# Two transfers per chunk instead of six for the last heads' rows, two closing stores on ScalarE, new planner numbers

## The chip, the cores and the metric

The kernel runs on one core of a Trainium2 chip. TensorE (PE in the profile) multiplies, VectorE (DVE) and ScalarE (ACT) work elementwise and empty PSUM, GpSimd (POOL) works elementwise on SBUF, SyncE (SP) issues nearly all transfers. The metric is the device time of one execution in microseconds, as the median of three runs. The kernel before took 326.67 us (326.44 to 327.48).

## The reference

Two computations in a row, for 4 batches of 768 positions. First a gated linear attention with 8 heads of 48 channels:

```
for t in range(S):
    state = alpha[:, :, t, :, None] * state + einsum('bhd,bhe->bhde', k[:, :, t], v[:, :, t])
    y[:, :, t] = einsum('bhd,bhde->bhe', q[:, :, t], state)
```

Its output, heads side by side (384 columns), is the input x of the second: four causal softmax attentions of width 64 ("experts"), each with its own wq, wk, wv, wo. A gate `x @ w_gate` picks two of the four for each position and weighs them.

```
scores = scale * (q @ k.transpose(0, 2, 1))          # causal mask, softmax -> a
ye = a @ v @ wo[e]
out += mask[..., None] * w[:, :, kk:kk + 1] * ye     # for the two experts chosen
```

## The kernel before

The sequence is cut into 24 chunks of 128 positions (6 for each batch). Three chunks make a unit u, two units a batch. A chunk n goes through these steps: SP loads alpha (`al`), q and k (`T`) and `v`; DVE turns alpha into running products with two scans (`prep_r`, `prep_c`, both through L163) and multiplies k and q with them (L182, L187); PE makes the products of the chunk (`gla_a`, L206), transposes k (`gla_t`, L223), makes the state's update (`gla_u`, L243) and the output (`gla_y`, L282). The masks between `gla_a` and `gla_y` are made either by DVE alone (L210) or by ACT and then POOL (L214, L218). A unit then goes through projections (`proj`, L305; `vproj`, L327), scores (L378), row maxima and exponentials (L390, L401), scaling on POOL (L413), transposes (L428), the product with v (L453) and the output product (`outp`, L472), whose result is copied to one of two `ot` tiles and stored (L480).

Heads lie in pairs on the partitions: one head on rows 0 to 47, the other on 64 to 111. From chunk 3 on (`FIRST = 3`) only three of the four pairs are loaded densely. The rows of the last two heads ride in the rows that are left over, 16 in each of three tiles, so that DVE prepares three tiles and not four. `spread` (L189) then moves them with transfers from SBUF to SBUF into their own, fourth tile: six transfers for each chunk, issued by SP (L194). PE's products of the fourth pair, and POOL's scaling of the state (L260), wait for them.

The order of all instructions is made by a planner at build time (`op` and `run`). Each step has a key, the steps it depends on, the engines that could do it with an assumed cost, and a target time. `run` takes, engine by engine, the step that can begin soonest, corrected by how far its target lies ahead. The targets come from PACE (assumed time of a chunk) and the shifts in OFF. Where a step may go to DVE or to another engine, the planner decides that too. Where it expects PE to be idle for longer than IDLE, it puts in filler products (`warm`, L805). So new numbers give a new order on every engine. Each queue runs strictly in its order: an instruction that waits holds back all behind it.

At the very end the count of a check (L856 to L864) decides whether a slow second path is taken; each engine loads it (`cnt`, TENSOR_LOAD at L864) before it goes on. On ACT this load stands ahead of the last copy of an output tile.

Of the kernel before, what the change touches and what calls it, by code (L numbers as in the profile page):

```python
# [17 lines left out]
B, H, S, D = 4, 8, 768, 48  # L18
DM = H * D
NE, HD = 4, 64  # L20
C = 128
# [9 lines left out]
TINY = 1.0e-12  # L31

FIRST = 3
PACE = 12.6339
PULL = {"P": 0.007, "V": 0.02, "A": 0.02, "G": 0.1134, "S": 0.1114}
SWITCH = 0.6006
CHANGE = {("t", "f"): 0.065, ("f", "t"): 0.0}
# [2 lines left out]
CHANGE.update({(x, "y"): 0.12 for x in "tfas"})  # L40
CHANGE.update({(x, "t"): 0.15 for x in "asy"})
CHANGE.update({(x, "f"): 0.2 for x in "asy"})
IDLE = 0.3068
SHARE = 0
HEAD = 0.0374
MARGIN = 0.3816
SLOW = 1.056
OFF = dict(load=1.5592, prep=0.7084, a=-0.2534, y=0.0569, p=-0.066, pw=0.4525, v=-0.5128, g=0.5234, s=-0.069, step=0.925, n=0.3117, tr=1.0059, o=0.1922, w=0.6642, wt=-1.9145, hp=1.0622, ck=0.4, end=1.3946, hd=0.0189, sx=-0.1743, wo=0.3118, xo=-0.0467)
UNITS = dict(a=7, at=4, ms=2, kt=2, x=2, q=3, k=4, yy=2, vg=3, T=4, al=3, v=3, ot=2, st=2)
HAND = {("P", "V"): 0.2, ("P", "A"): 0.2, ("P", "G"): 0.2, ("V", "P"): 0.1, ("A", "P"): 0.1, ("G", "P"): 0.14, ("S", "P"): 0.1,  # L50
        ("V", "G"): 0.07, ("A", "G"): 0.07, ("G", "V"): 0.07, ("G", "A"): 0.07}
# [4 lines left out]
def tile_gla_moe(ctx: ExitStack, tc: tile.TileContext, qk_d, al_d, v_d, wqk_d, wv_d, wo_d, nat_d, vn_d, out_d):  # L56
    nc = tc.nc
    V, A, G, PE, SY = nc.vector, nc.scalar, nc.gpsimd, nc.tensor, nc.sync
# [33 lines left out]
    wo = view(raw[2][:, 780:780 + 2 * DM], 2, DM)  # L92
# [66 lines left out]
    cq, ck = slice(0, 256), slice(256, 512)  # L159
# [29 lines left out]
    def spread(n):  # L189
        t = at(("T", n))  # L190
        for s in (0, 64):
            for i in range(3):
                r = s + 16 * i
                SY.dma_start(t[r:r + 16, 3, 0:2 * C + 1], t[s + D:s + 64, i, 0:2 * C + 1])  # L194

    def check(n):
        x = al(n).rearrange("p i a w -> p (i a w)") if n else raw[0][:, 0:8 * CW]
# [286 lines left out]
    def op(key, target, deps, alts, uses=(), take=(), mode="", land=0.0, lock=False):  # L484
        o = dict(key=key, target=target, deps=list(deps), alts=alts, uses=list(uses), take=list(take), mode=mode, land=land, lock=lock)
        ops.append(o)
        for n in o["uses"]:
            users[n] = users.get(n, 0) + 1
        return o
# [7 lines left out]
    def either(f, n, *a):  # L497
        return [("A", da(n), lambda: f("A", *a)), ("V", dv(n), lambda: f("V", *a))]

    def load_ops(n):  # L500
        z = (n - 3 - OFF["load"]) * PACE
        if n > HALF:
# [8 lines left out]
    def prep_ops(n):  # L511
        z = (n - 2 - OFF["prep"] + OFF["hp"] * max(0.0, 1.0 - (n - HALF) / 3) * (n >= HALF)) * PACE
        for i, (p0, p1) in enumerate(pieces(n)):
            k = p1 - p0
            past = [("c", n - 2, 0)] if n > 1 else []
            op(("r", n, i), z, [("La", n, i)] + past, [("V", 0.33 + 0.27 * k, lambda i=i: prep_r(n, i))], [("al", n)], lock=True)
            op(("e", n, i), z, [("r", n, i), ("Lq", n, i)], [("G", 0.19, lambda i=i: prep_e(n, i))], [("al", n), ("T", n)])
            op(("c", n, i), z, [("r", n, i)], [("V", 0.15 + 0.27 * k, lambda i=i: prep_c(n, i))], [("al", n)], lock=True)
            op(("k", n, i), z, [("r", n, i), ("Lq", n, i)], scale(prep_k, 128 * k, n, i), [("al", n), ("T", n)],
               lock=True)  # L520
            op(("q", n, i), z, [("c", n, i), ("Lq", n, i)], scale(prep_q, 128 * k, n, i), [("al", n), ("T", n)],
               lock=True)
        ready = [(x, n, i) for x in "ekq" for i in range(len(pieces(n)))]
        if n >= FIRST:
            op(("cp", n), z, ready, [("S", 3.45, lambda: spread(n))], [("T", n)], land=2.2)
            ready = [("cp", n)]
        op(("ck", n), z + OFF["ck"] * PACE, [(x, n, i) for x in "ekq" for i in range(len(pieces(n)))],
           [("A", 0.28 + 0.0021 * 129 * tiles(n) * 0.8, lambda: check(n))], [("al", n)])
        return ready

    def chunk_ops(n):
# [4 lines left out]
        head = OFF["hd"] if n < HALF else 0.0  # L536
        z = (n - 1 + OFF["a"] - head) * PACE
        op(("a", n), z, ready, [("P", 0.95, lambda: gla_a(n))], [("T", n)], [("pa", n, 0), ("pa", n, 1), ("ms", n)], "a")
# [5 lines left out]
        if not last:  # L544
            op(("t", n), z, ready, [("P", 0.42, lambda: gla_t(n))], [("T", n)], [("pt", n)], "t")
            op(("kt", n), z, [("t", n)], either(gla_k, 448, n), [("pt", n)], [("kt", n)])
        z = (n + OFF["y"] - head) * PACE
        op(("y", n), z, [("m", n, 0), ("m", n, 1), ("Lv", n)] + ([("S", n)] if c else []),
           [("P", 1.55 if c else 0.95, lambda: gla_y(n))], [("T", n), ("v", n), ("ms", n)], [("py", n)], "y")
        zx = z + OFF["xo"] * PACE  # L550
        op(("xh", n), zx, [("y", n)], [("A", da(W3), lambda: gla_xh(n))], [("py", n), ("x", u)], [("x", u)] if g == 0 else [])
# [39 lines left out]
    def back_ops(u):  # L591
        b, hf = divmod(u, 2)
        c = HALF * u + HALF
        tail = u == NU - 1
        step = (0.3333 + 0.3333 * hf) * OFF["step"]
        base = c + OFF["s"]
        seq = [(pair, i) for pair in (0, 1) for i in range(3)]
        for k, (pair, i) in enumerate(seq):
            tiles3 = [i] if hf else [0, 1, 2]
            first = hf or i == 0  # L600
            z = (base + step * k) * PACE
# [18 lines left out]
            for e in (0, 1):  # L620
                w = [c1 - c0 for c0, c1 in widths(u, i)]
                t = (u, pair, i, e)
# [5 lines left out]
            n = 128 * (3 * hf + i + 1)  # L628
            for e in (0, 1):
                t = (u, pair, i, e)  # L630
                op(("ns",) + t, z, [("n", u, pair, i), ("g3", u)], [("G", 0.35 + 0.00083 * n, lambda a=t: norm_s(*a))], [probs[e]])
            z = (base + step * k + OFF["tr"]) * PACE
            for e in (0, 1):
                t = (u, pair, i, e)
# [7 lines left out]
            if i == 2 or (tail and pair):  # L642
                for i0, i1 in ([(i, i + 1)] if tail and pair else [(0, 3)]):
                    z = (base + step * (k + 1) + OFF["o"]) * PACE
# [3 lines left out]
                    n = 128 * (i1 - i0)  # L648
                    y = ("yy", u, pair)
# [8 lines left out]
        for i in range(3):  # L658
            z = (base + step * 6 + OFF["w"] + 0.1 * i) * PACE
            op(("w", u, i), z, [("ol", u, 0, 0, 3), ("ol", u, 1, i, i + 1) if tail else ("ol", u, 1, 0, 3)],  # L660
               [("P", 1.06, lambda i=i: outp(u, i))], [("yy", u, 0), ("yy", u, 1)], [("po", u, i)], "f")
            end = tail and i == 2
            op(("wo", u, i), z, [("w", u, i)] + [("good",)] * end, either(outp_o, DM, u, i)[:1 if end else 2], [("po", u, i), ("ot", u, i)], [("ot", u, i)])
            op(("st", u, i), z, [("wo", u, i)], [("A", 0.4, lambda i=i: store(A, u, i)) if end else
                                                ("S", 0.57, lambda i=i: store(SY, u, i))], [("ot", u, i)], land=2.2)

# [31 lines left out]
    def run(start, arrive):  # L698
# [31 lines left out]
        while todo:  # L730
# [46 lines left out]
            alt[2]()  # L777
            dur = alt[1] * (SLOW if e in "VAG" else 1.0)
            end = t + dur
# [79 lines left out]
    z = (NG + 4) * PACE  # L859
# [5 lines left out]
    good = []  # L865
# [5 lines left out]
    with tc.If(good[0] == 0):  # L871
# [12 lines left out]
        for c in range(S // TT):  # L884
# [12 lines left out]
            for x in range(0, TT * D, 512):  # L897
                o = unit["g"][x // 512 % 8]
# [39 lines left out]
def _pack(q, k, v, alpha, w_gate, wq, wk, wv, wo):  # L938
    import numpy as np
    f = np.float32  # L940

    def pairs(x, fill, rev):
        x = x.reshape(B, 4, 2, NC, C, D)
        if rev:
            x = x[:, :, :, :, ::-1]
        x = x.transpose(0, 1, 2, 5, 3, 4)
        o = np.full((B, 4, 128, NC, C), fill, f)
        o[:, :, 0:D] = x[:, :, 0]
        o[:, :, 64:64 + D] = x[:, :, 1]
        for i in range(3):  # L950
            o[:, i, D:64] = x[:, 3, 0, 16 * i:16 * i + 16]
            o[:, i, 64 + D:128] = x[:, 3, 1, 16 * i:16 * i + 16]
        return o

    qf, kr, af, ar = pairs(q, 0, False), pairs(k, 0, True), pairs(alpha, 1, False), pairs(alpha, 1, True)
    qk = np.stack([x.transpose(0, 3, 2, 1, 4) for x in (qf, kr)], axis=4).reshape(NG, 128, 4, 2 * C)
    al = np.zeros((NG, 128, 2, 4, CW), f)
    for i, x in enumerate((af, ar)):
        al[:, :, i, :, 1:] = x.transpose(0, 3, 2, 1, 4).reshape(NG, 128, 4, C)
    vr = v.reshape(B, 4, 2, NC, C, D)[:, :, :, :, ::-1].transpose(2, 0, 3, 4, 1, 5)  # L960
    vp = np.zeros((B, NC, C, 4, 128), f)
    vp[..., 0:D] = vr[0]
    vp[..., 128 - D:128] = vr[1]
    vp = vp.reshape(B, NC, C, 512)
    nat = np.stack([x.reshape(B * H, S // 32, 32, 4, 12).transpose(1, 3, 0, 2, 4) for x in (alpha, k, q)], axis=3)
    nat = nat.reshape(S // 32, 128, 3 * 32 * 12)
    vn = v.reshape(B * H, S * D)
    rows = np.zeros((3, 4, 32), np.int64)
    for h in range(H):
        p, s = divmod(h, 2)  # L970
        rows[h // 4, h % 4] = h * D + 16 * s + np.arange(32)
        rows[2, p, 16 * s:16 * s + 16] = h * D + (32 if s == 0 else 0) + np.arange(16)
    rows = rows.reshape(3, 128)

    def wcols(*ws):
        w = np.concatenate(ws, axis=1)
        return np.ascontiguousarray(w[rows].transpose(1, 0, 2))

    wqk = wcols(*[wq[e] for e in range(NE)], *[wk[e] for e in range(NE)])
    wvg = wcols(*[wv[e] for e in range(NE)], w_gate)  # L980
    wop = np.ascontiguousarray(wo.reshape(2, 2 * HD, DM).transpose(1, 0, 2))
    return [np.ascontiguousarray(x) for x in (qk, al, vp, wqk, wvg, wop, nat, vn)]
# [27 lines left out]
```

## Time and profile before

| | us |
|---|---|
| median of 3 runs | 326.67 |
| profiled execution | 327.29 |
| its span, first to last instruction | 325.6 |
| PE busy | 310.3 |
| DVE busy | 266.6 |
| ACT busy | 196.9 |
| POOL busy | 129.5 |

The profiled execution lasts 327.29 us, of which 325.6 us lie between its first and last instruction. "Busy" of PE is a model: products overlap, and the end of each is worked out. A row of the timeline gives start and duration, and in brackets how long the engine sat idle before it and for what. The granted clock of PE was 1.00 in all slices but the last.

### The profile page before, as it was taken

The page shows a single profiled execution, that of the slowest core. Times are in us where ns is not written, and L with a number is a line of the kernel's source. Part 1 is how long each engine was busy: PE and PEld are TensorE (multiplying, and loading weights), DVE is VectorE, ACT ScalarE, POOL GpSimd, SP SyncE. Part 2 cuts the span into 40 slices and gives each one's busy share as a digit, 9 for nine tenths or more (in the row PEclk, how much of TensorE's full clock was granted, in tenths as well). Part 3 has the DMA queues.
Part 4 walks back from the last instruction along what each step waited for, and adds up shares of the span by engine and source line. Part 5 has one row for each costly group of instructions (what it writes and reads, how often), then busy time and mean ns, then how long its engine had stood idle before and what let it go on. Part 6 is the DMA issues. An engine that isn't in the chain of part 4 may idle for free.

```text
span 325.6 us, 11354 instructions
## 1 busy us (share of the span) xinstructions
PE 310.3 (95%) x4447; PEld 265.2 (81%) x4447; DVE 266.6 (82%) x754; ACT 196.9 (60%) x544; POOL 129.5 (40%) x202
## 2 busy tenths in 40 slices
PE   7799989999999999999999999999999999999992
PEld 5678877789887987889897987799897887878682
DVE  5998989999999899889899899599995785277740
ACT  1562655757665675656585777356584775457851
POOL 6353328512655073606455084205463072105320
PEclk9999999999999999999999999999999999999998
DMA  7994255373351321626353220713310000201001
GB/s 253 395 333 139 75 150 158 105 214 99 122 177 58 113 86 21 199 71 199 95 182 104 60 83 23 235 34 132 113 48 9 2 3 2 73 2 66 9 28 58
DMA packets 27982, 35.22 MB, mean 108 GB/s; under 512 B 3632, under 2 KB 24208, under 8 KB 27920
## 3 DMA queue, kind: packets, MB, share of 16 engines
q1 hardware_dynamic: 27232, 33.69, 32.5%
q8 instruction: 37, 0.61, 0.8%
q10 hardware_dynamic: 688, 0.72, 0.7%
q14 instruction: 25, 0.20, 0.2%
HBM read 27.61 MB, written 4.72 MB: 99 GB/s over the span
## 4 chain that ended last, share of the span: by engine, by line
PE 73%; DVE 13%; DMA 4%; ACT 2%; issue 2%; SPq 2%; POOL 1%; DVEq 0%; POOLq 0%; ACTq 0%
PE g L305 12%; PE g L428 11%; PE g L453 11%; PE g L378 9%; PE g L282 8%; PE g L472 7%; PE g L327 6%; PE g L206 5%; DVE al L163 2%; DMA T<-T 2%; PE g L243 2%; SPq L194 2%; DVE a L163 2%; PE g L223 2%; DVE T L182 1%
## 5 line engine op out<-in xcount | busy, mean ns | idle before, releaser
L413 POOL TENSOR_SCALAR a<-a,cf,gw 128x128 f32<-128x128 f32 (+5 forms) x96 | 75.4, 795 | 77.7 <-DVE cf L407 38.0
L401 ACT ACTIVATE a<-a,mx 128x256 f32<-128x256 f32 (+3 forms) x96 | 51.4, 538 | 7.0 <-DVE mx L390 6.9
L428 PE MATMUL g<-ident,a 128*128 128x128 f32 x336 | 52.6, 277 | 0.3
L305 PE MATMUL g<-x,wqkh 128*128 128x384 f32 x192 | 51.8, 350 | 0.3
L428 PEld LDWEIGHTS g<-ident,a 128*128 128x128 f32 x336 | 38.8, 140 | 7.9 <-issue 4.1
L227 ACT ACTIVATE at<-g 128x512 f32<-128x512 f32 (+3 forms) x79 | 34.9, 454 | 13.5 <-PE g L428 12.8
L218 POOL TENSOR_SCALAR_AFFINE_SELECT ms<-ms 128x512 f32<-128x512 f32 x25 | 18.0, 729 | 59.0 <-ACT ms L214 57.2
L453 PE MATMUL g<-at,vg 128*32 128x384 f32 (+2 forms) x648 | 40.2, 389 | 0.0
L378 PE MATMUL g<-k,q 64*128 64x256 f32 (+3 forms) x384 | 39.2, 336 | 0.0
L453 PEld LDWEIGHTS g<-at,vg 128*32 128x32 f32 x648 | 19.8, 110 | 18.5 <-issue 14.9
L282 PE MATMUL g<-ms,v 128*32 128x128 f32 x768 | 33.5, 274 | 0.9 <-DVE mx L390 0.4
L305 PEld LDWEIGHTS g<-x,wqkh 128*128 128x128 f32 x192 | 33.2, 189 | 1.1 <-DVE x L296 0.4
L378 PEld LDWEIGHTS g<-k,q 64*128 64x128 f32 x384 | 28.6, 185 | 5.8 <-issue 2.4
L327 PE MATMUL g<-wvh,x 128*128 128x260 f32 x144 | 31.9, 297 | 0.6 <-DVE mx L390 0.5
L305 PE MATMUL g<-x,wqkl 128*128 128x384 f32 x96 | 32.5, 338 | 0.0
L206 PE MATMUL g<-T 48*128 48x128 f32 x384 | 26.5, 277 | 3.3 <-DVE T L187 3.2
L229 DVE COPY at<-g 128x512 f32<-128x512 f32 (+3 forms) x49 | 24.0, 495 | 6.4 <-PE g L428 6.0
L390 DVE CUSTOM_DVE_ANT_0 a<-g,cmask 128x128 f32<-128x128 f32 (+3 forms) x64 | 28.0, 483 | 1.0 <-PE g L378 0.9
L206 PEld LDWEIGHTS g<-T 48*128 48x128 f32 x384 | 24.1, 188 | 5.3 <-DVE T L187 4.1
L472 PE MATMUL g<-woh,yy 128*128 128x384 f32 x96 | 27.3, 346 | 0.0
L260 POOL TENSOR_TENSOR S<-st,T 48x192 f32<-48x192 f32 x32 | 20.0, 626 | 17.4 <-DMA T<-T 6.5
L198 ACT ACTIVATE al<-al 128x774 f32<-128x774 f32 x21 | 17.8, 850 | 13.2 <-DVE T L187 10.3
(113 smaller groups left out, 636.8 us busy)
## 6 DMA issues: line engine op xcount, KB each, us to landing
al<-in_al_dram SPq DMA_DIRECT2D x21, 387.0 KB, 4.3
T<-in_qk_dram SPq DMA_DIRECT2D x21, 384.0 KB, 4.5
v<-in_v_dram SPq DMA_DIRECT2D x24, 256.0 KB, 3.4
out_dram<-ot SPq DMA_DIRECT2D x23, 192.0 KB, 1.9
T<-T SPq DMA_DIRECT2D x126, 16.1 KB, 1.9
a<-in_al_dram SPq DMA_DIRECT2D x2, 516.0 KB, 7.1
T<-in_qk_dram SPq DMA_DIRECT2D x2, 512.0 KB, 7.2
at<-in_wqk_dram SPq DMA_DIRECT2D x1, 768.0 KB, 9.2
```

Source lines behind the costliest of these rows:

```text
L206: PE.matmul(pa[s][:, C * p:C * p + C], t[r:r + D, p, C:2 * C], t[r:r + D, p, 0:C], start=True, stop=True, tile_position=(r, 0))
L227: A.activation(out, src, AF.Copy)
L282: PE.matmul(o[32 * j:32 * j + 32, k], l, r, start=(i == 0), stop=(i == len(parts) - 1), tile_position=(0, 32 * j))
L305: PE.matmul(pj[:, :W3], w[:, kt, cs], x[:, kt, :], start=(i == 0), stop=(i == 8))
L327: PE.matmul(pv[:, 0:260], x[:, kt, 128 * i:128 * i + 128], w[:, kt, :], start=(m == 0), stop=(m == 8))
L378: PE.matmul(sc(u, pair, i, e, x, c1 - c0), q[r, i0, ts], k[r, i1, c0:c1], start=(y == 0), stop=(y == 2), tile_position=(64 * e, 0))
L390: V.tensor_tensor_reduce(a[:, c0:c1], src, cmask[:, 512 - c1 + c0:512], -1.0, mx[:, 0:1] if x else 3.0e38, OP.add, OP.min, mx[:, 1:2])
L401: A.activation(a[:, c0:c1], src, AF.Exp, bias=mx[:, 1:2], scale=-1.0 if last else 1.0, accum_out=sm[:, x:x + 1])
L413: G.tensor_scalar(a[:, 0:n], a[:, 0:n], CF[u % 2][:, 3 * pair + i, e:e + 1], gw[:, u, i, eg:eg + 1], op0=OP.mult, op1=OP.mult)
L428: PE.transpose(pt[:, 128 * (j - j0):128 * (j - j0) + 128], a[:, 128 * j:128 * j + 128], ident)
L453: PE.matmul(o[r:r + 32, lo:n1], v[:, j % 3, 64 * eg + x:64 * eg + x + 32], at(("at", u, pair, e))[:, min(j, 4), at_off(j) + lo:at_off(j) + ...
L472: PE.matmul(po[:, 0:DM], y[:, h, 128 * i:128 * i + 128], w[:, pair, :], start=(m == 0), stop=(m == 5))
```

## The change

There are three edits. The first: `spread` issues two transfers for each chunk, one for each of the last two heads, and each moves 48 rows. The host packs these rows so that every third one lies in the same tile (`i::3` instead of blocks of 16), and one transfer with a plain order of rows does it. The planner's cost for the step on SP goes from 3.45 to 1.15 us. The second: of the last unit's three output tiles not only the last but the last two are copied by ACT and stored by ACT. The third: PACE, IDLE, HEAD, MARGIN, SLOW and some shifts in OFF have new values, so the order changes on all engines.

```
-PACE = 12.6339
+PACE = 12.4037
...
         for s in (0, 64):
-            for i in range(3):
-                r = s + 16 * i
-                SY.dma_start(t[r:r + 16, 3, 0:2 * C + 1], t[s + D:s + 64, i, 0:2 * C + 1])
+            SY.dma_start(t[s:s + D, 3, 0:2 * C + 1], t[s + D:s + 64, 0:3, 0:2 * C + 1])
...
-            op(("cp", n), z, ready, [("S", 3.45, lambda: spread(n))], [("T", n)], land=2.2)
+            op(("cp", n), z, ready, [("S", 1.15, lambda: spread(n))], [("T", n)], land=2.2)
...
-            end = tail and i == 2
-            op(("wo", u, i), z, [("w", u, i)] + [("good",)] * end, either(outp_o, DM, u, i)[:1 if end else 2], [("po", u, i), ("ot", u, i)], [("ot", u, i)])
+            end = tail and i > 0
+            op(("wo", u, i), z, [("w", u, i)] + [("good",)] * (end and i == 2), either(outp_o, DM, u, i)[:1 if end else 2], [("po", u, i), ("ot", u, i)], [("ot", u, i)])
...
-            o[:, i, D:64] = x[:, 3, 0, 16 * i:16 * i + 16]
-            o[:, i, 64 + D:128] = x[:, 3, 1, 16 * i:16 * i + 16]
+            o[:, i, D:64] = x[:, 3, 0, i::3]
+            o[:, i, 64 + D:128] = x[:, 3, 1, i::3]
```

The lines behind `spread` stand two lower in the new kernel (L192 for L194, L478 for L480); this text uses the numbers of before.

SP, chunks 3 to 5 (T_88, T_85, T_86 are their q and k tiles). Before:

```order
L109 DMA T_87<-in_qk_dram 128x3x256
L194 DMA T_88<-T_88 16x257 x6
L105 DMA al_89<-in_al_dram 128x2x387
L194 DMA T_85<-T_85 16x257 x6
L105 DMA al_90<-in_al_dram 128x2x387
L194 DMA T_86<-T_86 16x257 x6
```

And now:

```order
L109 DMA T_87<-in_qk_dram 128x3x256
L192 DMA T_88<-T_88 48x1x257 x2
L105 DMA al_89<-in_al_dram 128x2x387
L192 DMA T_85<-T_85 48x1x257 x2
L105 DMA al_90<-in_al_dram 128x2x387
L192 DMA T_86<-T_86 48x1x257 x2
```

The order there is the same, with two issues in each place instead of six; over the kernel 126 issues become 42.

DVE, the scans of chunk 3 (al_89; wol is the low part of the output weights). Before:

```order
L163 SCALAR_TENSOR_TENSOR al_89<-al_89,d1r 128x387
L169 RECIPROCAL d1c_110<-al_89 128x3
L163 SCALAR_TENSOR_TENSOR al_89<-al_89,d1c_110 128x387
L182 TENSOR_TENSOR T_88<-T_88,al_89 128x3x128
L187 TENSOR_TENSOR T_88<-T_88,al_89 128x3x128
```

And now:

```order
L163 SCALAR_TENSOR_TENSOR al_89<-al_89,d1r 128x387
L169 RECIPROCAL d1c_110<-al_89 128x3
L666 TENSOR_TENSOR wol<-at_65,woh 128x768
L163 SCALAR_TENSOR_TENSOR al_89<-al_89,d1c_110 128x387
L182 TENSOR_TENSOR T_88<-T_88,al_89 128x3x128
L187 TENSOR_TENSOR T_88<-T_88,al_89 128x3x128
```

The subtraction that makes wol came from POOL, where it stood beside these scans, to DVE between them.

ACT, the end of the main path (ot_95, ot_96 are the last two output tiles). Before:

```order
L459 ACTIVATE yy_81<-g_104 128x128
L227 ACTIVATE ot_95<-g_107 128x384
L864 TENSOR_LOAD cnt
L227 ACTIVATE ot_96<-g_106 128x384
L480 DMA out_dram<-ot_96 128x384
```

And now:

```order
L457 ACTIVATE yy_81<-g_107 128x128
L225 ACTIVATE ot_95<-g_105 128x384
L478 DMA out_dram<-ot_95 128x384
L862 TENSOR_LOAD cnt
L225 ACTIVATE ot_96<-g_102 128x384
L478 DMA out_dram<-ot_96 128x384
```

The store of ot_95 now stands between its copy and the load of the count, ahead of the last copy.

On PE the useful instructions are the same in number; the fillers (L805) go from 77 to 73. Of the places where the kind of product changes there were 295 in the main path and are now 302. In the stretch after the third value product of unit 0, five fillers and the products of chunk 3 (L206) follow at once, where a projection (L305) came first. The transposes of chunk 4 (L223) and its state update (L243) stand ahead of its products (L206), where the update came behind them. In the main path DVE makes 19 masks (23 before) and ACT with POOL 29 (25 before); 16 more copies out of PSUM go to DVE.

## Rows read from the trace of the kernel before

**Rows 1.** The page: busy time of each engine, and DVE's busy tenths in 40 slices
```profile
PE 310.3 (95%) x4447; PEld 265.2 (81%) x4447; DVE 266.6 (82%) x754; ACT 196.9 (60%) x544; POOL 129.5 (40%) x202
DVE  5998989999999899889899899599995785277740
```

**Rows 2.** Waits of PE: line, for whom, us in total, times, longest
```profile
PE g L223 <- DMA T<-T: 0.7, 1, 0.7
...
PE g L327 <- DVE mx L390: 0.5, 1, 0.5
```

**Rows 3.** Chain that ended last, one place in two batches: start, us, what
```profile
157.46 1.54 PE g L282 x56
...
231.18 1.54 PE g L282 x56
```

**Rows 4.** Timeline of PE, 33 to 63 us: start, us, instruction, idle before
```profile
33.24 0.52 PE L305 MATMUL g<-x,wqkh 128*128 128x384 f32 x2
...
34.84 0.72 PE L805 MATMUL g<-d1r 128*128 128x256 bf16 x5
35.49 1.71 PE L206 MATMUL g<-T 48*128 48x128 f32 x16
...
42.50 0.29 PE L223 MATMUL g<-ident,T 112*128 112x112 f32 x1 [0.72 <-DMA T<-T]
...
44.04 1.05 PE L206 MATMUL g<-T 48*128 48x128 f32 x16
45.78 0.54 PE L243 MATMUL g<-v,kt 128*32 128x48 f32 x32 [0.68 <-ACT ms L214]
46.25 1.16 PE L206 MATMUL g<-T 48*128 48x128 f32 x16
...
50.41 0.49 PE L805 MATMUL g<-d1r 128*128 128x256 bf16 x3
...
62.30 1.07 PE L282 MATMUL g<-ms,v 128*32 128x128 f32 x30 [0.23 <-POOL ms L218]
```

**Rows 5.** Timeline of SP's issues, 31 to 35 us
```profile
31.62 3.78 SPq L194 DMA_DIRECT2D T<-T  x6
```

**Rows 6.** Timeline of POOL, 27 to 37 us
```profile
27.99 1.82 POOL L668 TENSOR_TENSOR wol<-at,woh 128x768 fp32r<-128x768 f32 x1
...
36.76 0.70 POOL L260 TENSOR_TENSOR S<-st,T 48x192 f32<-48x192 f32 x1 [1.03 <-DMA T<-T]
```

**Rows 7.** Timeline of DVE, 22 to 34 us
```profile
22.54 0.95 DVE L668 TENSOR_TENSOR wqkl<-at,wqkh 128x768 fp32r<-128x768 f32 x1
...
28.03 2.61 DVE L163 TENSOR_TENSOR_SCAN al<-al,d1c 128x387 f32<-128x387 f32 x1
...
32.67 0.96 DVE L163 TENSOR_TENSOR_SCAN al<-al,d1c 128x387 f32<-128x387 f32 x1
```

**Rows 8.** Timelines of SP, ACT and PE around a unit's stores, 195 to 210 us
```profile
195.16 8.66 SPq L194 DMA_DIRECT2D T<-T  x12
...
208.64 0.49 ACT L227 ACTIVATE ot<-g 128x384 f32<-128x384 f32 x1 [3.38 <-DMA out_dram<-ot]
...
209.56 1.03 PE L305 MATMUL g<-x,wqkh 128*128 128x384 f32 x2
```

**Rows 9.** Timeline of ACT from 318 us, and ACT's load of the count
```profile
318.54 0.49 ACT L227 ACTIVATE ot<-g 128x384 f32<-128x384 f32 x1 [0.98 <-PE g L472]
319.58 0.49 ACT L227 ACTIVATE ot<-g 128x384 f32<-128x384 f32 x1 [0.55 <-PE g L472]
320.10 0.37 ACTq L480 DMA_DIRECT2D out_dram<-ot  x1
...
L864 ACTq TENSOR_LOAD <-cnt x1: 467/467/467, 318.6 to 318.6; - x1
```

**Rows 10.** POOL: all masks by line and form (count, busy, mean ns, idle), and one pair of scalings
```profile
L218 POOL TENSOR_SCALAR_AFFINE_SELECT ms<-ms 128x512 f32<-128x512 f32 x25 | 18.0, 729 | 59.0 <-ACT ms L214 57.2 <-DMA T<-in_qk_dram 1.8
...
311.05 1.95 POOL L413 TENSOR_SCALAR a<-a,cf,gw 128x768 f32<-128x768 f32 x2 [2.06 <-DVE at L229]
```

More of the change, by code (lines that the diff above doesn't have):

```diff
@@ L42 @@
 CHANGE.update({(x, "f"): 0.2 for x in "asy"})
-IDLE = 0.3068
+IDLE = 0.3647
 SHARE = 0
[L45 to L48, printed above, removed]
+HEAD = 0.0628
+MARGIN = 0.3762
+SLOW = 1.0555
+OFF = dict(load=1.5592, prep=0.7084, a=-0.2534, y=0.0569, p=-0.066, pw=0.4525, v=-0.5128, g=0.5234, s=-0.069, step=0.9176, n=0.3117, tr=1.0059, o=0.2201, w=0.7913, wt=-1.9145, hp=1.0622, ck=0.6172, end=1.3946, hd=0.1337, sx=-0.1614, wo=0.0629, xo=-0.1397)
 UNITS = dict(a=7, at=4, ms=2, kt=2, x=2, q=3, k=4, yy=2, vg=3, T=4, al=3, v=3, ot=2, st=2)
```

## The prediction

> **What bounds the kernel now.** I read the page first, then PE's waits, the chain that ended last, and then the timelines of the places that these name. The page has PE busy for 310.3 of the span's 325.6 us [rows 1]. The chain is almost all PE from about 35 us on. One and the same place stands in it at 157.46 and, one batch of six chunks later, at 231.18 us [rows 3]: 73.72 us for a batch in which hardly any wait of PE is printed. So the middle of the kernel lasts as long as PE's products do, and the change leaves their number as it is. What it can win is only what PE spends waiting or on fillers, and that is little: the list of PE's waits is short [rows 2], and the largest losses lie between 33 and 63 us [rows 4], where the first chunks with a moved fourth tile pass. DVE stands second. Its digits are nines in most slices of the first two thirds [rows 1], so PE can run ahead there only as far as DVE lets it.
>
> **The early stretch, 33 to 51 us.** Before, SP issued the six transfers of chunk 3 from 31.62 us on, in 3.78 us [rows 5], that is 0.63 us each, so the last left at 35.40. The second half was in place when POOL's step that waited for it began, at 36.76 [rows 6], 1.36 us later. Two transfers take 1.26 us of issue, so the last leaves 2.52 us earlier. How long one of 48 rows takes to land no row shows; I bound it by the same 1.36 us from below and by that plus the whole 2.52 us saved from above, and take the lower end with some tenths on top, since that row is the same kind of transfer with the same row length.
>
> DVE comes to that point sooner too. A scan took 2.61 us at 28.03, and the next one of the same kind 0.96 at 32.67 [rows 7]. While the long one ran, POOL made wol from 27.99 to 29.81 [rows 6]. Now DVE makes wol itself, for 0.95 us, the time of the same operation at 22.54 [rows 7]. DVE gains 1.65 and pays 0.95: 0.70 us. So chunk 3's rows leave SP for good at about 35.40 - 2.52 - 0.70 = 32.2 and are there by 34.
>
> PE's losses in this stretch: the products of chunk 3 took 1.71 us at 35.49 and took 1.16 at 46.25 without a wait, so 0.55 is a wait in their midst; the transpose at 42.50 waited 0.72 for the transfers, and the state update at 45.78 waited 0.68 [rows 4]. The new order puts the projection behind chunk 3's products and the transposes and the update of chunk 4 ahead of its own products, each with 1 to 3 us of other work before it. I let all three go: 0.55 + 0.72 + 0.68 = **-1.95 us**; if the landing is at its upper end the first comes back. The five fillers at 34.84 (0.72 us) stand in the new order as well, so they stay.
>
> **51 to 63 us.** Three fillers at 50.41 (0.49 us) are gone from the order, and an output product that waited 0.23 us for POOL's mask at 62.30 [rows 4] now has a whole chunk's worth of other products between itself and the products it depends on. Both go if DVE keeps up: **-0.7 us** (0 if it doesn't).
>
> **Later waits.** Twelve issues of SP in a row took 8.66 us from 195.16 on, the unit's stores stood behind them, and ACT waited 3.38 us for a free output tile; PE's projection at 209.56 then took 1.03 us for two products, where two took 0.52 at 33.24 [rows 8, 4]. Now four issues stand there, 2.5 us, and the stores leave some 6 us earlier: **-0.5 us**. Of the 0.5 us that PE waited for DVE's maxima [rows 2] I take half: **-0.25**.
>
> **What it adds.** First, PE changes the kind of product 302 times and not 295. The products of a chunk took 1.05 us at 44.04, behind scores of the same row layout, and 1.16 at 46.25, behind another kind [rows 4]: 0.11 for a change, **+0.8 us** for seven. The bounds are 0 and 1.6.
>
> Second, the end. The last copies of ACT began at 318.54 and 319.58, the latter when PE had finished; its load of the count, 0.47 us, ran beside the first copy, and the last store's issue took 0.37 [rows 9]. Now a store stands ahead of the load. It can only be issued when the first copy is done, at 319.03; 0.37 and 0.47 behind one another end at 319.87, and the last copy begins then or shortly after in place of 319.58: **+0.4 us** with the hand-over. The bounds are 0 (the load overlaps) and 0.84. SP is rid of one issue, but the end doesn't hang on SP: its last store left before ACT's. The Trainium skill (DMA: Bandwidth & Descriptors, Issuing engines are not separate DMA queues) says that a transfer runs on the same engines whoever issues it, and only issue time is saved. By that rule the edit has nothing to give at the end; without it one could hope for the 0.4 back. No run here shows a store of this size from both engines at one moment.
>
> Third, a new order makes new waits. I take **+0.3**, between 0 and 3.6 (below).
>
> The sum is -1.95 - 0.7 - 0.5 - 0.25 + 0.8 + 0.4 + 0.3 = -1.9 us. The profiled execution (span 325.6, 327.29 in all, 0.62 above the median) would come to 325.4, the median from 326.67 to **324.8 us**. The 84 issues that SP loses cost nothing elsewhere: where it is idle it waits for others, and only the places above show anyone waiting for it.
>
> **Rivals.** *Gains given back to DVE.* DVE is full through most of the first 230 us [rows 1], and the order gives it 16 more copies and wol, against four masks and the 1.65 us. If PE meets DVE a few us later, it waits there for what it won; then only the end and the changes remain, with part of the start: 326.2 to 327, say 326.5. For it: the nines. Against it: PE's waits for DVE after 60 us are half a microsecond in all [rows 2], so DVE has some slack. If the merged transfer lands late, the time falls in the same place, 1 us nearer to before.
>
> *More of it goes.* The new numbers clear all waits named, the fillers at 34.84 too, and no new ones come: -1.95 - 0.72 - 0.7 - 0.5 - 0.5 and the changes at half price, +0.4, the end +0.4: -3.6, 323.1 us. For it: an earlier fourth tile relaxes everything behind it. Against it: the fillers are still in the order.
>
> *Slower: masks on POOL.* Four masks move from DVE to ACT and POOL. A mask on POOL takes 0.73 us [rows 10], and queues behind pairs of scalings, 1.95 us for a pair at the full width [rows 10]; PE's output product needs both masks. If each of the four waits for half a pair, about 1 us, and PE with it, that is +4 in place of +0.3: 326.67 - 1.9 + 3.6 = 328.4 us. It decides from about 0.6 us for each mask on. For it: PE did wait for such a mask [rows 4], 0.23 us. Against it: POOL stood idle 59 us before masks [rows 10], which is the opposite of a queue. The Trainium skill (SBUF, Who interferes with whom) makes POOL's work dearer still: an elementwise DVE instruction with two SBUF inputs and a POOL instruction that reads SBUF exclude each other, and the later one waits the other out. The long scan agrees: POOL's 29.81 plus some 0.8 is the scan's end at 30.64. By that rule four more masks of 0.73 could hold DVE up by 2.9 us, which is within this rival's price.
>
> **How the numbers follow.** About 0.3% (1 us) is what a measurement of this kernel can tell from no change. Forecast -1 to -3 us: 0.45. More of it goes, below 323.7: 0.20. Given back, within 1 us: 0.20. Slower: 0.15, of which the masks most. So faster 0.65, same 0.20, slower 0.15. The forecast's own range is 323.7 to 325.7; with half of the case above it and of the one beyond no change on either side, the range is 322.2 to 327.5.
>
> **What would show it.** The products of chunk 3 should begin near 34 us and last 1.1 to 1.2; no wait of PE for T<-T should be left; the first transposes of unit 0 should begin 2 us before 50.20 or earlier; the scan of chunk 3 should take 0.96 behind a wol of 0.95; ACT's wait of 3.38 us should be gone; the gap between ACT's last two copies should grow to about 0.9. I am wrong if a batch in the middle takes over 74.3 us in place of 73.72, or if PE's list of waits gets entries for POOL's masks or DVE that come to more than 2 us.

## The result, and the profile after

The changed kernel takes **322.1 us** (median of 4 runs, 321.5 to 322.3) where the kernel before took 327.1 beside it (4 runs): a ratio of 0.984, 95% interval 0.980 to 0.988, or 5.0 us less. Repeated later it was 322.2 (6 runs), ratio 0.984 [0.981, 0.987]. The forecast, 324.8 us, had the sign right and less than half of the size, and the time lies 0.1 us below the range. Lines of the new kernel are two lower than those of before from L194 on.

The page after, engines and DVE's tenths, as in [rows 1]:

```profile
PE 307.3 (96%) x4443; PEld 264.2 (82%) x4443; DVE 266.7 (83%) x767; ACT 195.3 (61%) x532; POOL 125.2 (39%) x205
...
DVE  4997999999999999898998899898795785767840
```

DVE is as full as before. The gain is in PE: 3 us less busy, since fewer of its products stretch over a wait. Its list of waits (line, for whom, us, times, longest), the whole of it, against [rows 2]:

```profile
PE g L204 <- DVE T L187: 4.2, 4, 1.6
PE g L803 <- POOL ones L137: 1.5, 1, 1.5
PE g L241 <- issue: 1.0, 1, 1.0
PE g L426 <- DVE at L227: 0.4, 1, 0.4
PE g L325 <- DVE mx L388: 0.3, 1, 0.3
```

The first three lie ahead of 26 us. The fourth is new: at 190.87 us PE waits for a copy by DVE (below). No wait for T<-T and none for a mask is left. Timeline of PE (start, us, instruction, idle before), against [rows 4]:

```profile
33.66 0.72 PE L803 MATMUL g<-d1r 128*128 128x256 bf16 x5
34.30 1.16 PE L204 MATMUL g<-T 48*128 48x128 f32 x16
...
47.73 0.39 PE L325 MATMUL g<-wvh,x 128*128 128x260 f32 x1 [0.34 <-DVE mx L388]
...
48.91 0.27 PE L426 MATMUL g<-ident,a 128*128 128x128 f32 x1
...
57.58 1.06 PE L280 MATMUL g<-ms,v 128*32 128x128 f32 x32
58.57 0.33 PE L426 MATMUL g<-ident,a 128*128 128x128 f32 x1
...
61.72 0.55 PE L221 MATMUL g<-ident,T 112*128 112x112 f32 x4
62.11 0.38 PE L426 MATMUL g<-ident,a 128*128 128x128 f32 x2
...
86.00 0.98 PE L376 MATMUL g<-k,q 64*128 64x512 f32 x6
86.92 0.33 PE L426 MATMUL g<-ident,a 128*128 128x128 f32 x1
```

Chunk 3's products last 1.16 us in place of 1.71. Unit 0's first transpose comes at 48.91, 1.3 us earlier, where 2 were foreseen. SP, POOL and DVE, against [rows 5 to 7]:

```profile
31.10 1.35 SPq L192 DMA_DIRECT2D T<-T  x2
...
28.30 0.94 DVE L666 TENSOR_TENSOR wol<-at,woh 128x768 fp32r<-128x768 f32 x1
29.16 0.96 DVE L163 TENSOR_TENSOR_SCAN al<-al,d1c 128x387 f32<-128x387 f32 x1
...
33.51 2.03 POOL L258 TENSOR_TENSOR S<-st,T 48x192 f32<-48x192 f32 x2 [1.35 <-DMA T<-T]
```

The scan beside wol takes 0.96 as foreseen, and a 48-row transfer lands in 2.2 us (median of 42; a 16-row one took 1.9). The chain has the place of [rows 3] twice as well:

```profile
153.26 1.54 PE g L280 x56
...
226.60 1.62 PE g L280 x56
```

That is 73.34 us for the batch (73.72 before): the lead is 4.20 us at the first place and 4.58 at the second, so nearly all of it was won ahead of 153 us, and some 0.45 is left to the end.

To see where, I priced each form of product by its usual distance from start to start in the trace of before (some 280 us in all) and compared when both kernels had done the same product work; this is an estimate, good to a few tenths. The new one leads by 1.3 us at 50 us of before's time, 1.7 at 60, 3.0 at 65, 3.5 at 70, 4.4 at 100, 4.3 at 150, 4.5 at 310 and 5.0 at the span's end. Fillers and waits between 55 and 101 us come to some 3 us less than before: **3 of the 5 us lie where the forecast had hardly looked.** The profile of the repeated run (`after_again`) has a lead of 0.8 at 50 us and 4.2 at 100, so the same 3 us and more in that stretch.

The end, ACT, against [rows 9]:

```profile
313.98 0.49 ACT L225 ACTIVATE ot<-g 128x384 f32<-128x384 f32 x1 [0.98 <-PE g L470]
...
315.53 0.49 ACT L225 ACTIVATE ot<-g 128x384 f32<-128x384 f32 x1 [1.06 <-PE g L470]
316.05 0.78 ACTq L478 DMA_DIRECT2D out_dram<-ot  x1
```

The last copy comes 1.55 us behind the one ahead of it (1.04 before): the added 0.5 us is there. Yet from the last store's issue to the end of the span only 4.5 us pass (320.5 - 316.05), where it was 5.5 (325.6 - 320.10).

### The profile page after: what moved, and what is told of

It reads as the page before. It is cut to its first block, busy times and chain, and to the rows that moved or that the text cites. A ratio compares the mean times of both kernels' runs of the same rounds, so it can differ in the third digit from the quotient of the medians.

```text
span 320.5 us, 11175 instructions
## 1 busy us (share of the span) xinstructions
PE 307.3 (96%) x4443; PEld 264.2 (82%) x4443; DVE 266.7 (83%) x767; ACT 195.3 (61%) x532; POOL 125.2 (39%) x205
## 4 chain that ended last, share of the span: by engine, by line
PE 83%; DVE 11%; DMA 2%; issue 1%; ACT 1%; POOL 0%; ACTq 0%; SPq 0%; DVEq 0%; POOLq 0%
PE g L303 15%; PE g L426 12%; PE g L451 12%; PE g L376 9%; PE g L280 9%; PE g L325 8%; PE g L470 8%; PE g L204 5%; PE g L241 2%; PE g L221 2%; DMA at<-in_al_dram 2%; DVE a L388 2%; DVE a L163 2%; DVE T L187 1%; DVE T L182 1%
## 5 line engine op out<-in xcount | busy, mean ns | idle before, releaser
L411 POOL TENSOR_SCALAR a<-a,cf,gw 128x128 f32<-128x128 f32 (+5 forms) x96 | 72.6, 767 | 78.8 <-DVE cf L405 28.7
L216 POOL TENSOR_SCALAR_AFFINE_SELECT ms<-ms 128x512 f32<-128x512 f32 x29 | 21.0, 733 | 56.0 <-ACT ms L212 56.0
L225 ACT ACTIVATE at<-g 128x512 f32<-128x512 f32 (+3 forms) x68 | 31.2, 473 | 17.1 <-PE g L426 15.7
L227 DVE COPY at<-g 128x256 f32<-128x256 f32 (+3 forms) x60 | 27.6, 467 | 9.2 <-PE g L426 8.6
L204 PE MATMUL g<-T 48*128 48x128 f32 x384 | 26.7, 277 | 4.2 <-DVE T L187 4.2
L212 ACT ACTIVATE ms<-g 128x512 f32<-128x512 f32 x29 | 16.4, 591 | 14.8 <-PE g L204 14.4
```

The costliest lines, as they stand in the source:

```text
L204: PE.matmul(pa[s][:, C * p:C * p + C], t[r:r + D, p, C:2 * C], t[r:r + D, p, 0:C], start=True, stop=True, tile_position=(r, 0))
L225: A.activation(out, src, AF.Copy)
L411: G.tensor_scalar(a[:, 0:n], a[:, 0:n], CF[u % 2][:, 3 * pair + i, e:e + 1], gw[:, u, i, eg:eg + 1], op0=OP.mult, op1=OP.mult)
```

## Experiments

A ratio is to the kernel before on the same chip. "Old order" and "new order" mean that each engine's order is that of before, or of the changed kernel, exactly.

**Transfers and order apart.** `two_old`: before, with the new `spread` and packing, the planner's cost left at 3.45.

> The kernel before with two transfers per chunk in place of six; every engine's order is exactly that of before, only SP has 84 issues fewer. Theory A (the refitted order gives most of the 5 us, since it takes PE's waits on DVE away between 50 and 100 us; the transfers only open the way): 0.5 to 1.3 us below before, that is 0.9960 to 0.9985 of its time, almost all of it between 33 and 47 us, where PE waits 0.72 for T<-T and 0.55 within the products of chunk 3. Theory B (the early landing of the fourth tile gives most of it, and relaxes everything behind): 2.5 to 4 us below, 0.988 to 0.992. Theory C (neither gives anything without the other): within 0.5 us.

325.7 us, 0.997 [0.995, 0.999]; repeated as `two_again`, 325.8, 0.996 [0.993, 0.998], with the changed kernel (`after_again`, told above) beside it.

> Two transfers alone in before's order, once more, as the measure of the two above: 325.7 us, 0.997 of before.

> The changed kernel once more, as the measure of the runs in the new order: 322.1 us, 0.984 of before.

`six_new`: the changed kernel with the old `spread` and packing.

> The changed kernel with six transfers per chunk and the old packing; every engine's order is exactly the new one. Theory A: 3 to 4.3 us below before (0.987 to 0.991); T<-T comes 2.5 us later than with two transfers, so PE's wait for it is back by 0.7 to 2 us near 33 to 45 us, the rest stays. Theory B: at most 1.5 us below before (over 0.995). Theory C: the new order stands the first products of chunk 3 earlier behind transfers that are no earlier: within 1 us of before.

332.1 us, 1.015 [1.013, 1.017]. None of the three theories fits both runs: the time of `two_old` lies in the range of theory A, but more than half of its gain comes at 205 us (below) and not by 47, and `six_new` is slower than before by 5 us, which none foresaw. Two transfers give 1 to 1.5 us in the old order and 10 in the new; the new order gives 3.6 us with two transfers and costs 5 with six. The two parts only work together. PE's waits with six:

```profile
PE g L223 <- DMA T<-T: 4.9, 5, 2.4
...
PE g L206 <- DMA T<-T: 1.7, 2, 1.2
```

```profile
41.70 0.29 PE L223 MATMUL g<-ident,T 112*128 112x112 f32 x1 [2.38 <-DMA T<-T]
```

6.6 us for T<-T: the new order puts products right behind the rows that two transfers bring in time. A part of the rest is the clock: behind the 2.4 us wait the granted clock was 0.66 over 42 to 47 us, with 0.50, the lower level of 1.2 GHz, from 43 to 46; in the changed kernel it was 1.00 over 42 to 47. The products from the state update to the next projection took 5.04 us there (41.91 to 46.95) against 3.45 in the changed kernel (37.91 to 41.36), 1.6 us more.

In the old order the lead of two transfers is 0.3 us from 50 to 205 us (from -0.4 at the products of chunk 3, 35.91 for 35.49, its opening being later; counted from there, 0.7 is won early) and 1.3 from 220 on. The second step is the stall of [rows 8], in `two_again`:

```profile
194.86 4.26 SPq L192 DMA_DIRECT2D T<-T  x4
...
204.82 0.48 ACT L225 ACTIVATE ot<-g 128x384 f32<-128x384 f32 x1
```

ACT's copy comes at 204.82 in place of 208.64, without its 3.38 us wait: 1.0 us for PE, where 0.5 was forecast.

**The planner's cost alone.** `two_replan`: as `two_old`, but with the cost at 1.15, so that the old numbers make a new order.

> The kernel before with two transfers per chunk and the planner told of their cost (1.15 us for 3.45), all other numbers as before, so the planner makes its own order from the old numbers. Theory E (the planner only had to know the shorter transfer; the refitted numbers are of no weight): 322 to 323.5 us, as the changed kernel. Theory F (the refitted numbers make the order, the cost alone does not): 325 us or more, no better than two transfers in the old order (325.7).

327.3 us, 0.999 [0.996, 1.002]: theory F. That order led by 2.5 us at 70 us and then lost it, 1.7 of it in one wait of scores for an output copy, and more behind that wait, where the granted clock was 0.50 over 82 to 84 us:

```profile
79.01 0.61 PE L376 MATMUL g<-k,q 64*128 64x256 f32 x5 [1.66 <-ACT ot L225]
```

**What six issues cost in the new order.** `pad_last` and `pad_first`: four idle transfers behind, or ahead of, the two:

```
+        for i in range(4):
+            SY.dma_start(scr[n % 2][i][:, 0:C + 1], d1r[32 * i:32 * i + 16, 0])
```

> The changed kernel with four idle transfers (16 rows of 129 elements between two tiles that nothing uses) behind the two of each chunk, so SP issues six again, the useful rows first; all orders are else the same. Theory G (what six transfers cost in the new order, 332.1 against 322.1 us, is that the fourth tile's rows leave SP 2.5 us later): 322 to 324 us. Rival H (it is that SP is busy 3.7 us per chunk, so loads, stores and the next chunk's rows behind come late): 328 us or more.

> The same with the four idle transfers ahead of the two useful ones. Theory G: 329 to 333 us, as with six useful transfers in the new order. Rival H: the same as with the idle ones behind. PE's waits for T<-T should come back by 4 us or more (6.6 us with six useful ones) by G.

325.4 us, 0.994 [0.992, 0.997], and 327.5 us, 1.001 [0.998, 1.003]. Neither theory gives the times: four more transfers behind the useful ones cost 3.2 us, and that the rows leave later 2.2 more. PE's waits for T<-T in `pad_first` come to 4.2 us, as theory G said. What the 3.2 us come from, SP's issue time or the traffic itself, these runs don't tell apart, and 332 isn't reached; the idle transfers carry half the bytes of the real ones. The profiled execution of `pad_last` shows how a wait can be multiplied (clock is the third figure from the end). It took 328.75 us, 3.4 above the median, and its mean clock was 0.984; in nine of the twelve executions, all at 325.9 us or less, it was 0.988 to 0.998:

```profile
51.39 0.32 PE L224 MATMUL g<-ident,T 112*128 112x112 f32 x1 [0.88 <-DMA T<-T]
```

```profile
52.00:58.00 6.00, 6.00 (x72) 4.70 (x72) 4.47 (x11) 2.63 (x7) 4.41 (x7) 0.65 0.57 179
```

**Is it DVE?** `new_wol2` makes wol twice on DVE in the new order (28 us); `dve8` and `dve14` add two idle products behind the first scan of chunk 8 (60 us) or 14 (131 us); `old_dve8` does so at chunk 8 in the old order:

```
-        return [("V", 0.96, lambda: f(V)), ("G", 1.75, lambda: f(G))]
+        return [("V", 0.96, lambda: (f(V), f(V))), ("G", 1.75, lambda: f(G))]
...
+        if n == 8:
+            for _ in range(2):
+                V.tensor_tensor(scr, d1r[:, 0:3, 0:C], d1r[:, 0:3, 0:C], OP.mult)
```

> The changed kernel with wol made twice on DVE, one directly behind the other (0.95 us of idle work added at 28 us); all orders are the same. Theory D: 0.7 to 0.95 us later, about 322.9 to 323.1. Rival (PE sets the pace, DVE has slack at the opening): at most 0.3 us later.

323.1 us, 0.987 [0.985, 0.988]: 1.0 later. DVE does set the pace at the start: from the start of chunk 3's first scan to DVE's first maxima it is 18.61 us (26.71 to 45.32) in place of 17.62 (27.22 to 44.84), and PE waits for these maxima in both kernels.

> The changed kernel with two idle products on DVE (128x384, 0.55 us each, on a tile that nothing uses) behind the first scan of chunk 8, at about 60 us; all orders are else the same. Theory D (DVE sets the pace up to about 100 us): 0.7 to 1.1 us later than the changed kernel, 322.8 to 323.2. Rival (PE sets the pace from about 50 us on): at most 0.3 later.

> The same two idle products behind the first scan of chunk 14, at about 131 us, where DVE waits now and then (0.80 us at 129.21 in the changed kernel). Theory D says nothing of this stretch; with PE setting the pace there: at most 0.3 us later than the changed kernel. If DVE set the pace all through: 0.7 to 1.1 later.

322.0 us, 0.984 [0.980, 0.987], and 321.7 us, 0.983 [0.979, 0.986]: 1.1 us more on DVE costs nothing at 60 or at 131 us, so theory D falls there.

> The kernel before with two transfers, in before's order, and two idle products on DVE (128x384, 0.55 us each) behind the first scan of chunk 8, at about 63 us. Theory K (in the old order DVE sets PE's pace from 62 to 100 us, and the new order gave DVE slack there): 0.8 to 1.1 us later than two transfers alone, where the same edit cost nothing in the new order. Rival L (the losses of PE at 61.7, 87.3 and 96.0 us come from the place of single instructions in DVE's and POOL's queues, and DVE as a whole has slack in the old order too): at most 0.3 us later.

325.9 us, 0.997 [0.994, 1.000], against 325.8: nothing in the old order either. Theory K falls, though DVE's digits there are nines. The reverse, `old_skip8` (`if n != 8:` ahead of the products of `prep_k` and `prep_q`):

> The same kernel without the two products that scale q and k of chunk 8 on DVE (1.0 us at 64.6; the result is no longer the reference's). Theory K: 0.7 to 1.1 us earlier than two transfers alone, the losses of PE at 87.3 and 96.0 us gone. Rival L: within 0.3 us of it.

326.6 us, 0.998 [0.995, 1.000]; as a time it tells nothing, since half of its runs had a mean granted clock under 0.99. But the places of 87.3 and 96.0 us tell. With the edit:

```profile
89.45 0.96 PE L378 MATMUL g<-k,q 64*128 64x512 f32 x6
90.84 0.43 PE L282 MATMUL g<-ms,v 128*32 128x128 f32 x8 [0.43 <-DVE mx L390]
...
98.21 0.60 PE L223 MATMUL g<-ident,T 112*128 112x112 f32 x4
99.35 0.39 PE L327 MATMUL g<-wvh,x 128*128 128x260 f32 x1 [0.54 <-DVE mx L390]
```

They last 1.39 and 1.14 us from start to start, to the hundredth as without it. The three places in `two_again` (two transfers, old order):

```profile
61.26 0.41 PE L280 MATMUL g<-ms,v 128*32 128x128 f32 x2
62.00 1.07 PE L280 MATMUL g<-ms,v 128*32 128x128 f32 x30 [0.33 <-POOL ms L216]
63.01 0.55 PE L426 MATMUL g<-ident,a 128*128 128x128 f32 x3
...
86.95 0.95 PE L376 MATMUL g<-k,q 64*128 64x512 f32 x6
88.34 0.43 PE L280 MATMUL g<-ms,v 128*32 128x128 f32 x8 [0.44 <-DVE mx L388]
...
95.72 0.60 PE L221 MATMUL g<-ident,T 112*128 112x112 f32 x4
96.86 0.39 PE L325 MATMUL g<-wvh,x 128*128 128x260 f32 x1 [0.53 <-DVE mx L388]
```

From start to the start of the next kind: 1.75, 1.39 and 1.14 us. The same products in the changed kernel (above) take 0.99, 0.92 and 0.39. So **the three lose 0.76, 0.47 and 0.75 us, where the idle printed in brackets is 0.33, 0.44 and 0.53**: the rest lies within the modelled duration of what stands ahead. In `old_dve8` the second place is at 86.13, in time as long as ever:

```profile
86.13 0.96 PE L380 MATMUL g<-k,q 64*128 64x512 f32 x6
87.52 0.42 PE L284 MATMUL g<-ms,v 128*32 128x128 f32 x8 [0.43 <-DVE mx L392]
```

A chain makes the last two, by the printed releaser: PE waits until DVE's maxima free a PSUM tile, and neither more nor less work on DVE at chunk 8 changed that. The new order has other products in those places. Rival L stands; which of the new numbers put them there was not tried.

**wol between DVE and POOL.** `old_woldve`: two transfers, old order, wol emitted by DVE where POOL had it (`("G", 1.75, lambda: f(V))`); `new_wolpool`: the reverse in the new order (`("V", 0.96, lambda: f(G))`).

> The kernel before with two transfers, in before's order, and wol made by DVE in the same place instead of POOL. Theory D: the long scan (2.61) takes 0.96, DVE pays 0.95, and 0.5 to 0.8 us are gained over two transfers alone (325.7): about 325.0. Rival (PE sets the pace): within 0.2 us of 325.7.

325.1 us, 0.994 [0.992, 0.996]: 0.6 us better than two transfers alone in medians (the intervals overlap), 1.1 by the lead in the profiles, of which 0.5 is the later opening of `two_again`; and the scan takes 0.96 again.

> The changed kernel with one instruction on another engine: wol (the low part of the output weights) is made by POOL in the same place of the program, as before the change; all other orders are the same. Theory D (DVE, not PE, sets the pace from about 28 to 100 us, and the new order gains because DVE is stretched less by POOL: 5.1 us of stretching in 26 to 101 us before, 1.5 after): the scan beside wol goes from 0.96 back to about 2.6 us, DVE is rid of 0.95, so the end comes 0.7 us later, about 322.8. Rival (PE sets the pace, and the gain is the waits of PE named in the prediction): within 0.2 us of the changed kernel, since PE has a wait of 1.0 us for nothing else there.

322.1 us, 0.983 [0.982, 0.984]: no loss. wol now ran earlier on POOL, from 25.38 to 27.20, and the scan that began at 26.74 took 1.28 us and not 2.6. It ended 0.82 us behind POOL, as the long scan of before did (0.83), so the two met here too, but for 0.46 us only. DVE, rid of 0.6 us, won nothing.

**The fillers at 33 us.** `lean_after` and `lean_pool`: the changed kernel and `new_wolpool` without the five fillers (`warm(i, k if len(fills) != 6 else 0)`, the sixth call).

> The changed kernel with wol made by POOL, and without the five filler products that stand ahead of chunk 3's products (33.2 us, 0.65 us); all orders are else the same. Theory M (with wol on DVE, DVE and PE are about level from 28 to 50 us; with wol on POOL, PE alone sets the pace, and there the fillers stand in its way, since chunk 3's rows are in place by 33.1 us): 0.5 to 0.7 us below the changed kernel, about 321.5, the best of all. Rival N (the products then wait for the rows, or what is won is lost to DVE at once): within 0.3 us of 322.1.

> The changed kernel without the same five fillers (wol stays on DVE). Theory M: at most 0.3 us below the changed kernel, since DVE is 0.6 us later than with wol on POOL and PE would wait for it. Rival (DVE isn't in the way, PE alone sets the pace): 0.5 to 0.7 us below, as in the other one.

322.0 us, 0.985 [0.982, 0.987], and 322.7 us, 0.986 [0.983, 0.988]: no gain in either. The first is rival N's. The second is above the changed kernel by 0.5, which neither theory foresaw; its six executions spread from 321.4 to 323.0, so little hangs on it. In `lean_pool` PE leads by 0.45 us more than in `new_wolpool` up to 45 us and has lost it by 50:

```profile
45.29 1.29 PE L204 MATMUL g<-T 48*128 48x128 f32 x16
47.07 0.39 PE L325 MATMUL g<-wvh,x 128*128 128x260 f32 x1 [0.48 <-DVE mx L388]
```

This is the place of 47.73 in the changed kernel: there PE waits for DVE's first maxima. What PE wins ahead of 47 us beyond a few tenths ends in this wait, and what DVE loses ahead of it (the second wol) ends in the time.

**The end.** `notail`: the changed kernel with `end = tail and i == 2`; `tail_only`: before with the new end.

> The changed kernel with the old end: only the last of the three stores on ScalarE, the one before it on SyncE; nothing else in the order differs. Theory A on the end (SP's closing steps were late because SP issued and then awaited its own store; without it the span ends sooner behind the last store): 0.4 to 0.6 us above the changed kernel, about 322.6. Rival (the prediction's: the issue and the load ahead of the last copy cost 0.4, and SP's end hides nothing): 0.4 us below the changed kernel, about 321.7. In the profile, the time from PE's last instruction to the span's end should be near 6.1 us by the first, 5.6 in the changed kernel.

> The kernel before with nothing but the new end: the last two stores on ScalarE. Theory A on the end: 0.3 to 0.6 us below before (0.998 to 0.999), PE's last instruction to the span's end 5.6 us in place of 6.1. Rival (the prediction's price): 0.4 us above before (1.001).

322.4 us, 0.986 [0.984, 0.988], and 327.6 us, 1.000 [0.998, 1.002]: too little for the times, which also differ in sign (the old end 0.3 us above the changed kernel, the new end 0.4 above before). The profiles tell it apart: from the start of PE's last product to the span's end it is 6.3 to 6.6 us in all eight profiles with the old end, and 5.4 to 6.2 in eleven of twelve with the new one (6.45 in the twelfth). So by the profiles the edit gives about 0.5 us at the end, the later last copy included; as a time it is not shown. SP's closing waits (8 of 17 ns) run from 323.6 to 324.2 in the kernel before and from 314.0 to 318.8 in the changed one. That they made the end late fits; it was not tried alone.

## Why the prediction was too small

The 5.0 us come in these stretches, by the lead: 1.3 by 50 us, 3.1 from there to 100, 0.1 from there to 310, and 0.5 at the end.

- *33 to 51 us, -1.95*: about right, near the low side. Waits for T<-T and for the state's masks went as described; 1.3 us were won by 50 us, 1.7 counted from 26.7 us, where the new order started 0.4 later. In `after_again` DVE began chunk 3 0.45 us later, and 0.8 were won by 50 us. The place at 47 us, where PE waits for DVE, took the rest: the mechanism of the first rival, with a small price.
- *51 to 63 us, -0.7, and half of PE's wait for DVE's maxima, -0.25*: **this is the step that failed.** From 50 to 100 us 3.1 us were won. I went by the idle printed beside two waits, 0.23 us at 62.30 and 0.5 for DVE's maxima, and booked 0.48 for both. And I wrote that the waits for DVE after 60 us are half a microsecond in all; the full list behind [rows 2] has one more. The list's line and the three places in the kernel before:

```profile
PE g L282 <- DVE mx L390: 0.4, 1, 0.4
```

```profile
61.67 0.41 PE L282 MATMUL g<-ms,v 128*32 128x128 f32 x2
62.30 1.07 PE L282 MATMUL g<-ms,v 128*32 128x128 f32 x30 [0.23 <-POOL ms L218]
63.30 0.55 PE L428 MATMUL g<-ident,a 128*128 128x128 f32 x3
...
87.25 0.95 PE L378 MATMUL g<-k,q 64*128 64x512 f32 x6
88.64 0.43 PE L282 MATMUL g<-ms,v 128*32 128x128 f32 x8 [0.44 <-DVE mx L390]
...
96.02 0.61 PE L223 MATMUL g<-ident,T 112*128 112x112 f32 x4
97.15 0.39 PE L327 MATMUL g<-wvh,x 128*128 128x260 f32 x1 [0.52 <-DVE mx L390]
```

  By the distances from start to start the first is worth 0.64 us (63.30 - 61.67 for 32 products, 0.99 after), the last 0.74, and the one at 87.25, which I had left out, 0.47: 1.85 us, all gone in the new order. The other 1.2 lie in the three fillers (0.49, booked) and in places of 0.3 and less. That these waits would go was right for two of them; their price was too small, and the stretch from 63 to 100 us was taken as all but free of losses.
- *Stores, -0.5*: the mechanism is right, worth 1.0 us in the old order. The stores left SP 2.7 us earlier there (201.96 for 204.62) and not 6, since the four issues took 4.26 us and not 2.5. In the changed kernel ACT's wait is gone too, but the lead is 4.4 at 100 and 4.5 at 310 us: most of the gain is lost again, the largest piece in the new wait below.
- *Seven more kind changes, +0.8*: not seen. Between 55 and 101 us PE loses 3 us less with them, and from 100 to 310 us the lead doesn't fall. Their number told nothing.
- *The end, +0.4*: the copy is 0.5 later as worked out, but behind the last issue 1.0 us less passes. "The end doesn't hang on SP" is the half that looks wrong: I looked at who issued last, not at what SP still did. The rule of the Trainium skill (DMA: Bandwidth & Descriptors, Issuing engines are not separate DMA queues), that a transfer gains nothing by another issuer, isn't contradicted: what was measured is the span's end, and no run shows the same store from both engines at one moment.
- *New waits, +0.3*: there is one, for a copy by DVE:

```profile
189.88 0.60 PE L221 MATMUL g<-ident,T 112*128 112x112 f32 x4
190.87 0.30 PE L426 MATMUL g<-ident,a 128*128 128x128 f32 x1 [0.39 <-DVE at L227]
```

  By starts it costs 0.6 us (0.99 for four transposes that took 0.39 at 61.72), so here the term was mis-sized by 0.3. The slower rival, masks on POOL, didn't occur: 29 masks of 733 ns on POOL and no wait of PE for one. The rule of the Trainium skill on DVE and POOL (SBUF — State Buffer, Who interferes with whom) holds where they meet: with wol on DVE the scan of 2.61 us took 0.96 in both orders, as two instructions that exclude each other would.

## What to carry to other kernels

Take a wait's price from the distance between the starts of two instructions, against the same pair elsewhere in the trace, and not from the idle printed before the second: here three places lost 1.85 us, of which the prediction had booked 0.48. A cheaper step and an order fitted to it belong together: each alone was worth 1.5 us or less than nothing, both together 5. That an engine is nine tenths busy says little on whether it sets the pace: 1 us of added work cost 1.0 us at 28 us and nothing at 60 or 131.

## What the runs showed of the hardware

- A 48-row, 48 KB transfer from SBUF to SBUF lands in 2.2 us, three of 16 rows in 1.8 to 1.9 each; both take 0.6 us to issue. Per row the long one is three times as cheap for the issuer.
- A wait of PE can cost more than itself. In four profiles the granted clock fell to 0.50 (1.2 GHz) for 2 us or more soon behind waits of PE: 2.38 us in `six_new`, 0.88 in `pad_last`, 1.66 in `two_replan`, 0.78 and 0.48 in `old_skip8`. Not each wait does that: behind 1.16 us at 36.44 in `six_new` and 1.45 at 38.82 in `pad_last` it stayed at 1.00 until the next one.
- Which of DVE and POOL comes first can differ between executions of one kernel. In `after` DVE's subtraction for wqkl began at 22.67 us and took 0.95; POOL's for wvl began at 23.30, while it ran, and took 2.04. In `after_again` POOL began first, at 23.31, and took 1.91; DVE began at 23.43 and took 2.61, and its first scan of chunk 3 came 0.45 us later.
